# Linear attention with a two-layer MLP: two heads side by side as 64-wide tiles of the TensorE array

## The chip, the cores and the metric

One core of one Trainium2 chip. The metric is the device time of the whole program in microseconds, as the median of several runs. Runs are compared in the state called fast; runs that lay more than 1.5% above the fastest of their kernel are called slow, and neither the medians nor the ratios below include them. The sessions of experiments ran on different chips, so a ratio is always against runs of the kernel before in the same session, and a difference between medians of two sessions is rougher than a ratio.

## The reference, cut to what matters

Blockwise linear attention (batch 4, 8 heads, 768 positions, head size 64) carries a 64x64 state per batch and head. Its output goes through two matrix products with a gated activation between them.

```python
for b in range(nb):
    intra = np.einsum('bhic,bhjc->bhij', qb, kb) * Dmask[None]
    intra = np.einsum('bhij,bhjd->bhid', intra, vb)
    inter = np.einsum('bhid,bhde->bhie', qb * lam_pow[None], kv_state)
    out[:, :, sl] = intra + inter
    kv_state = lam_block[...] * kv_state + np.einsum('bhsd,bhse->bhde', kb_dec, vb)
...
x = attn_out.transpose(0, 2, 1, 3).reshape(B * S, H * D)     # 3072 x 512
h = x @ w_in                                                  # 512 -> 2048
return (h * (1.0 / (1.0 + np.exp(-1.702 * h)))) @ w_out       # 2048 -> 512
```

## The kernel before

The sequence is cut into six windows of 128 positions, 0 to 5. In each window the attention of the next window runs on TensorE between the MLP matmuls of the current one. Window 0 and 1 work in units of one batch and four heads (`u_` functions), windows 2 to 5 in pairs of heads over all four batches (`p_` functions). Two heads of 64 fill the 128 partitions.

```python
def hd(h):
    return slice(64 * h, 64 * h + 64)
...
v_sb = [const.tile([P, NP, B, 3, D], bf16, ...) for i in range(2)]   # v of head 0, zeros, v of head 1
kv_sb = [const.tile([P, NP, B, P], bf16, ...) for i in range(2)]     # states: two 64x64 blocks on the diagonal, zeros else
...
def p_score(w, p):                       # 64-row matmuls, one per head
    ...
    nc.tensor.matmul(s[:, h, b, :], t[hd(h), 0, b, :], t[hd(h), 1, b, :], start=True, stop=True)

def p_kv(w, p):                          # full width: computes both heads' blocks and two unused ones
    ...
    for b in range(B):
        nc.tensor.matmul(t[:, b, :], ks[:, 0, b, :], v_sb[w % 2][:, p, b, 0:3:2, :], start=True, stop=True)
    for h in range(2):                   # the two diagonal blocks, 64 partitions each
        nc.vector.scalar_tensor_tensor(new[hd(h), p, :, hd(h)], old[hd(h), p, :, hd(h)], ..., t[hd(h), :, hd(h)], ...)

def p_out(w, p):                         # full width: the zeros of kv_sb keep the heads apart
    ...
    for b in range(B):
        nc.tensor.matmul(o[:, b, :], kq_of[w, p][:, 1, b, :], kv_sb[w % 2][:, p, b, :], start=True, stop=True)   # inter
        for h in range(2):
            nc.tensor.matmul(o[:, b, hd(h)], sm[:, h, b, :], v_sb[w % 2][:, p, b, 2 * h, :], start=False, ...)   # intra

def u_out(w, b, g):                      # window 1: the same with the operands swapped, 128 columns moving
    ...
    if w:
        nc.tensor.matmul(o[:, p, :], kv_sb[w % 2][:, pp, b, :], kq_of[w, b][:, 1, pp, :], start=True, stop=False)
    for h in range(2):                   # v with a block of zeros beside it
        nc.tensor.matmul(o[:, p, :], v_sb[w % 2][:, pp, b, h : h + 2, :]..., sm[:, h, p, :], ...)
```

## Time and profile before

| | before |
|---|---|
| median of 3 runs | 223.77 us (223.6 to 223.9) |
| profiled span | 222.9 us |
| TensorE (PE) busy | 93% of the span |
| VectorE (DVE), ScalarE (ACT) busy | 41%, 43% |

From the page of the kernel before come the busy times (us, share of the span, number of instructions) and, from its part 4, the chain of work that ended last, by engine:

```profile
PE 208.3 (93%) x1476; PEld 109.0 (49%) x1476; DVE 92.0 (41%) x218; ACT 95.1 (43%) x202; POOL 35.9 (16%) x57
...
PE 74%; DMA 13%; SPq 4%; POOL 3%; DVE 3%; issue 1%; ACT 0%; DVEq 0%; ACTq 0%
```

TensorE bounds the kernel. Of the DMA part of the chain (13%), 11% belong to the first 42 us, in which inputs and weights arrive. The other 2% are the transposing DMA of one output, at 83.5 to 88.1 us. What TensorE waits for after that, from the view of waits between 42 us and the end:

```profile
PE ps_o L337 <- ACT xs L342: 1.6, 1, 1.6
PE ps_t L227 <- DVE kqs L206: 0.6, 1, 0.6
PE ps_s L311 <- DVE sm L318: 0.6, 1, 0.6
PE ps_kv L326 <- DVE kv L329: 0.5, 1, 0.5
PE ps_t L227 <- POOL kqs L206: 0.3, 1, 0.3
```

The columns are the total, the number of waits and the longest. These waits come to 3.6 us in 181 us, and they all lie before 89 us.

The timeline shows what one piece of attention costs. The columns are start, length, engine, line, operation, operands, shape and number. This is one output call (`p_out`) of window 3:

```profile
109.55 1.03 PE L358 MATMUL ps_h<-xT,w_in 128*128 128x512 bf16 x4
110.41 0.22 PE L337 MATMUL ps_o<-kv,kq 128*128 128x128 bf16 x1
110.47 0.22 PE L339 MATMUL ps_o<-v_sb,sm 128*128 128x64 bf16 x2
110.52 0.22 PE L337 MATMUL ps_o<-kv,kq 128*128 128x128 bf16 x1
...
110.86 0.81 PE L358 MATMUL ps_h<-xT,w_in 128*128 128x512 bf16 x3
```

Read the starts, not the lengths: the matmuls overlap in this view, and their ends are modelled by the profiler. From start to start, 128 moving columns take about 56 ns, 64 columns 28 ns and 512 columns 216 ns. The call of 12 matmuls takes 0.45 us. "128\*128" is the part of the array in use, rows by columns. Figures in ns here and below are differences of starts in the packed trace, which has them to 1 ns; the view rounds to 10.

The same view of scores and state matmuls of one pair of heads:

```profile
104.34 0.59 PE L358 MATMUL ps_h<-xT,w_in 128*128 128x512 bf16 x2
104.87 0.40 PE L311 MATMUL ps_s<-kq 64*128 64x128 bf16 x8
105.20 0.40 PE L326 MATMUL ps_kv<-v_sb,kqs 128*128 128x128 bf16 x4
105.43 0.59 PE L358 MATMUL ps_h<-xT,w_in 128*128 128x512 bf16 x2
```

The two MLP matmuls from 104.34 us fill the array until 104.34 + 2 x 0.216 = 104.77 us, but the scores (64 rows) start at 104.87 us. About 0.1 us is empty although nothing is waited for, and the same happens from the scores to the state matmuls. From the state matmuls (128\*128) to the MLP there is no such hole. In what follows such a change of the array's shape is called a passage.

One output call of window 1 (`u_out`) and its two state matmuls, all of one shape:

```profile
55.77 0.22 PE L284 MATMUL ps_o<-kq,kv 128*128 128x128 bf16 x1
55.83 0.27 PE L287 MATMUL ps_o<-sm,v_sb 128*128 128x128 bf16 x2
...
56.11 0.28 PE L262 MATMUL ps_kv<-v_sb,kqs 128*128 128x128 bf16 x2
56.22 0.60 PE L358 MATMUL ps_h<-xT,w_in 128*128 128x256 bf16 x4
```

### The profile page before, as it was taken

The page shows a single profiled execution, that of the slowest core. Times are in us where ns is not written, and L with a number is a line of the kernel's source. Part 1 is how long each engine was busy: PE and PEld are TensorE (multiplying, and loading weights), DVE is VectorE, ACT ScalarE, POOL GpSimd, SP SyncE. Part 2 cuts the span into 40 slices and gives each one's busy share as a digit, 9 for nine tenths or more (in the row PEclk, how much of TensorE's full clock was granted, in tenths as well). Part 3 has the DMA queues.
Part 4 walks back from the last instruction along what each step waited for, and adds up shares of the span by engine and source line. Part 5 has one row for each costly group of instructions (what it writes and reads, how often), then busy time and mean ns, then how long its engine had stood idle before and what let it go on. Part 6 is the DMA issues. An engine that isn't in the chain of part 4 may idle for free.

```text
span 222.9 us, 3886 instructions
## 1 busy us (share of the span) xinstructions
PE 208.3 (93%) x1476; PEld 109.0 (49%) x1476; DVE 92.0 (41%) x218; ACT 95.1 (43%) x202; POOL 35.9 (16%) x57
## 2 busy tenths in 40 slices
PE   7687999699899987999999999999999999999993
PEld 2354344145784675444555444554444545444452
DVE  0792000246588984163654183572372432100121
ACT  5996662244771344146522056612076421366000
POOL 4879300232211001011020120110120000000000
PEclk9999999889999999999999999999999999999999
DMA  6999999899988797889774999747793122200112
GB/s 136 245 206 148 205 206 219 189 232 234 222 187 268 170 238 159 184 222 195 174 167 131 225 239 196 163 109 192 177 252 75 26 84 80 94 3 0 47 47 94
DMA packets 109638, 35.91 MB, mean 161 GB/s; under 512 B 102324, under 2 KB 106676, under 8 KB 109620
## 3 DMA queue, kind: packets, MB, share of 16 engines
q1 hardware_dynamic: 105236, 31.47, 60.7%
q0 software_dynamic: 4240, 4.19, 11.8%
q8 instruction: 11, 0.18, 0.4%
q14 instruction: 7, 0.06, 0.1%
q10 hardware_dynamic: 144, 0.00, 0.0%
HBM read 27.27 MB, written 6.29 MB: 151 GB/s over the span
## 4 chain that ended last, share of the span: by engine, by line
PE 74%; DMA 13%; SPq 4%; POOL 3%; DVE 3%; issue 1%; ACT 0%; DVEq 0%; ACTq 0%
PE ps_out L379 34%; PE ps_h L358 29%; DMA w_out<-in_moe_w_out_dram 7%; DMA qf<-in_q_dram 4%; SPq L82 4%; DMA xT<-xs 2%; PE ps_s L311 2%; POOL w_in L161 2%; PE ps_o L337 2%; PE ps_out L397 2%; PE ps_o L339 2%; PE ps_kv L326 2%; POOL kqs L206 1%; PE ps_t L227 1%; PE ps_s L246 1%
## 5 line engine op out<-in xcount | busy, mean ns | idle before, releaser
L358 PE MATMUL ps_h<-xT,w_in 128*128 128x512 bf16 (+1 forms) x448 | 88.5, 349 | 1.5 <-DMA w_in<-in_moe_w_in_dram 1.5
L379 PE MATMUL ps_out<-w_out,g_sb 128*128 128x512 bf16 x368 | 86.0, 384 | 0.0
L364 ACT ACTIVATE g_sb<-ps_h 128x512 bf16<-128x512 f32 (+1 forms) x112 | 59.5, 537 | 60.2 <-PE ps_h L358 59.2
L358 PEld LDWEIGHTS <-w_in 128*128 128x128 bf16 x448 | 42.1, 98 | 38.9 <-DMA w_in<-in_moe_w_in_dram 2.2
L379 PEld LDWEIGHTS <-g_sb 128*128 128x128 bf16 x368 | 34.5, 98 | 37.9 <-issue 1.0
L386 DVE COPY o_sb<-ps_out 128x512 f32<-128x512 f32 x19 | 13.1, 691 | 56.8 <-PE ps_out L379 50.2
L318 DVE TENSOR_TENSOR sm<-ps_s,dmask 128x512 bf16<-128x512 f32 x32 | 20.6, 686 | 26.9 <-PE ps_s L311 26.9
L300 POOL CAST v_sb<-vf 128x512 bf16<-128x512 f32 x16 | 12.3, 767 | 100.1 <-DMA vf<-in_v_dram 90.4
L342 ACT CAST xs<-ps_o 128x512 bf16<-128x512 f32 x16 | 9.4, 586 | 25.6 <-PE ps_o L339 23.2
L206 DVE TENSOR_TENSOR kqs<-kf,k_pow 128x256 bf16<-128x256 f32 x16 | 7.5, 469 | 27.6 <-DMA kf<-in_k_dram 23.3
L206 POOL TENSOR_TENSOR kqs<-qf,q_pow 128x256 bf16<-128x256 f32 x16 | 10.2, 641 | 29.4 <-DMA qf<-in_q_dram 26.6
L251 DVE TENSOR_TENSOR sm<-ps_s,dmask 128x512 bf16<-128x512 f32 x16 | 11.1, 691 | 5.3 <-PE ps_s L246 4.8
L329 DVE SCALAR_TENSOR_TENSOR kv<-kv,blk_pow,ps_kv 64x256 bf16<-64x256 bf16 x24 | 11.4, 476 | 0.2
L337 PE MATMUL ps_o<-kv,kq 128*128 128x128 bf16 x64 | 9.0, 220 | 1.6 <-ACT xs L342 1.6
L289 ACT CAST xT<-ps_o 128x256 bf16<-128x256 f32 x16 | 6.0, 375 | 9.7 <-PE ps_o L287 9.5
L298 DVE TENSOR_SCALAR kqs<-kf,k_pow 128x256 bf16<-128x256 f32 x32 | 9.8, 349 | 0.2
L298 DVE TENSOR_SCALAR kqs<-qf,q_pow 128x256 bf16<-128x256 f32 x32 | 9.8, 348 | 0.0
L274 DVE SCALAR_TENSOR_TENSOR kv<-kv,blk_pow,ps_kv 64x64 bf16<-64x64 bf16 x32 | 7.7, 279 | 4.9 <-PE ps_kv L262 4.5
L227 PE MATMUL ps_t<-ident,kqs 128*128 128x128 bf16 x64 | 6.8, 220 | 3.2 <-DVE kqs L206 2.5
L339 PEld LDWEIGHTS <-sm 128*128 128x128 bf16 x128 | 7.9, 98 | 3.2 <-issue 1.8
L211 ACT CAST v_sb<-vf 128x256 bf16<-128x256 f32 x16 | 6.4, 401 | 7.1 <-DMA vf<-in_v_dram 6.9
L339 PE MATMUL ps_o<-v_sb,sm 128*128 128x64 bf16 x128 | 9.0, 193 | 0.0
(54 smaller groups left out, 111.7 us busy)
## 6 DMA issues: line engine op xcount, KB each, us to landing
kf<-in_k_dram SPq DMA_DIRECT2D x48, 128.0 KB, 2.9
qf<-in_q_dram SPq DMA_DIRECT2D x48, 128.0 KB, 3.0
vf<-in_v_dram SPq DMA_DIRECT2D x48, 128.0 KB, 3.0
out_dram<-o_sb SPq DMA_DIRECT2D x23, 256.0 KB, 2.7
w_out<-in_moe_w_out_dram POOLq DMA_DIRECT2D x4, 512.0 KB, 15.8
w_in<-in_moe_w_in_dram POOLq DMA_DIRECT2D x3, 512.0 KB, 9.4
w_in<-in_moe_w_in_dram POOLq DMA_DIRECT2D x2, 256.0 KB, 5.6
kq<-kqs SPq DMA_TRANSPOSE x16, 3.5
```

Of the source, the lines that this page charges most:

```text
L206: eng.tensor_tensor(out.rearrange("s p h d -> s (p h) d"), xf.rearrange("s p h d -> s (p h) d"), tab, op=MUL)
L251: nc.vector.tensor_tensor(sm, s_ps.pop((w, b, g)).rearrange("s h (p t) -> s h p t", t=P)[:, :, 0:2, :], dmask[:, :, gs(g), :], op=MUL)
L298: nc.vector.tensor_scalar(kqs[:, i, :, h, :], loaded[w, "kq"[i], p][:, :, h, :], scalar1=(k_pow, q_pow)[i][:, 2 * p + h : 2 * p + h + 1], ...
L300: nc.gpsimd.tensor_copy(v_sb[w % 2][:, p, :, 0:3:2, :], loaded[w, "v", p])
L318: nc.vector.tensor_tensor(sm[:, h], s[:, h], dmask[:, h, p : p + 1, :].to_broadcast([P, B, P]), op=MUL)
L329: nc.vector.scalar_tensor_tensor(new[hd(h), p, :, hd(h)], old[hd(h), p, :, hd(h)], blk_pow[hd(h), 2 * p + h : 2 * p + h + 1], t[hd(h), :, ...
L337: nc.tensor.matmul(o[:, b, :], kq_of[w, p][:, 1, b, :], kv_sb[w % 2][:, p, b, :], start=True, stop=True)
L339: nc.tensor.matmul(o[:, b, hd(h)], sm[:, h, b, :], v_sb[w % 2][:, p, b, 2 * h, :], start=False, stop=True, skip_group_check=True)
L358: nc.tensor.matmul(t[:, bs[0] * P : bs[1] * P], w_in_sb[j][:, kc, i * P : (i + 1) * P], xT(w)[:, kc, bs[0] : bs[1], :].rearrange("p b t -> ...
L364: nc.scalar.activation(g_tile(w)[:, fc, c], h_ps.pop((w, fc))[:, c], GELU)
L379: nc.tensor.matmul(t, g_of[w][:, fc, g * P : (g + 1) * P], w_out_sb[j][:, fc % CW, :], start=(fc == 0), stop=(fc == FFC - 1))
L386: nc.vector.tensor_copy(o, t)
```

## The change

The intent is to stop multiplying by zeros. States are kept as compact 64x64 blocks, one head in each half of the partitions. The inter product runs as two 64-row matmuls, one per head. State matmuls become two 64-column tiles. The zeros in `v_sb` and `kv_sb` and the four memsets that write them vanish, and VectorE updates both heads' states in one instruction. The Trainium skill, TensorEngine Tiling (Array Packing), Gotcha 1: PSUM Pressure, says that row tiles cannot access one PSUM bank at the same time. So the output of windows 2 to 5 takes two banks, one per head, and the state result shares a bank with the transposes.

```diff
-    v_sb = [const.tile([P, NP, B, 3, D], bf16, name=f"v_sb{i}") for i in range(2)]
-    kv_sb = [const.tile([P, NP, B, P], bf16, name=f"kv{i}") for i in range(2)]
+    v_sb = [const.tile([P, NP, B, 2, D], bf16, name=f"v_sb{i}") for i in range(2)]
+    kv_sb = [const.tile([P, NP, B, D], bf16, name=f"kv{i}") for i in range(2)]
 ... (u_kv and u_kv_up: like p_kv below)
 def u_out(w, b, g):
             if w:
-                nc.tensor.matmul(o[:, p, :], kv_sb[w % 2][:, pp, b, :], kq_of[w, b][:, 1, pp, :],
-                                 start=True, stop=False)
-            for h in range(2):
-                nc.tensor.matmul(o[:, p, :], v_sb[w % 2][:, pp, b, h : h + 2, :].rearrange("p c d -> p (c d)"),
-                                 sm[:, h, p, :], start=(not w and h == 0), stop=(h == 1))
+                for h in range(2):
+                    nc.tensor.matmul(o[hd(h), p, :], kv_sb[w % 2][hd(h), pp, b, :], kq_of[w, b][hd(h), 1, pp, :],
+                                     start=True, stop=False)
+            for h in range(2):
+                nc.tensor.matmul(o[hd(h), p, :], v_sb[w % 2][:, pp, b, h, :], sm[:, h, p, :], start=not w, stop=True)
 def p_kv(w, p):
-        for b in range(B):
-            nc.tensor.matmul(t[:, b, :], ks[:, 0, b, :], v_sb[w % 2][:, p, b, 0:3:2, :], start=True, stop=True)
-        ... (two scalar_tensor_tensor of 64 partitions)
+        for b in range(B):
+            for h in range(2):
+                nc.tensor.matmul(t[hd(h), b, :], kqs_of[w, p][:, 0, b, h, :], v_sb[w % 2][:, p, b, h, :],
+                                 start=True, stop=True)
+        nc.vector.scalar_tensor_tensor(kv_sb[(w + 1) % 2][:, p], kv_sb[w % 2][:, p], blk2[:, p : p + 1], t, ...)
 def p_out(w, p):
-            nc.tensor.matmul(o[:, b, :], kq_of[w, p][:, 1, b, :], kv_sb[w % 2][:, p, b, :], start=True, stop=True)
-            for h in range(2):
-                nc.tensor.matmul(o[:, b, hd(h)], sm[:, h, b, :], v_sb[w % 2][:, p, b, 2 * h, :], ...)
+            for h in range(2):
+                nc.tensor.matmul(o[:, h, b, :], kq_of[w, p][hd(h), 1, b, :], kv_sb[w % 2][hd(h), p, b, :],
+                                 start=True, stop=True)
+            for h in range(2):
+                nc.tensor.matmul(o[:, h, b, :], sm[:, h, b, :], v_sb[w % 2][:, p, b, h, :],
+                                 start=False, stop=True, skip_group_check=True)
 ... (window 1: state matmuls a quarter step later than the output; memsets removed; bank layout)
```

More of the change, by code (lines that the diff above doesn't have):

```diff
@@ L208, in u_cast_v @@
     def u_cast_v(w, b, g, eng):
-        out, xf = v_sb[w % 2][:, gs(g), b, 0:3:2, :], loaded[w, "v", b][:, gs(g)]
+        out, xf = v_sb[w % 2][:, gs(g), b, :, :], loaded[w, "v", b][:, gs(g)]
         if eng is nc.scalar:
@@ L223, in u_turn @@
         if (w, b, g) not in t_ps:
-            t_ps[w, b, g] = ps.tile([P, 2, 2, P], bf16, tag="t", name="ps_t")
+            t = ps.tile([P, 8, P], bf16, tag="t" if w else "mm", bufs=1 if w else 3, name="ps_t")
+            t_ps[w, b, g] = t[:, 0:4, :].rearrange("s (i p) t -> s i p t", i=2)
         src = kqs_of[w, b].rearrange("s i p h d -> s i p (h d)")
@@ L257, in u_kv @@
     def u_kv(w, b, g):
-        t = ps.tile([P, 2, P], f32, tag="kv", name="ps_kv")
+        t = ps.tile([P, W], f32, tag="t", bufs=1, name="ps_kv")[:, 0 : 2 * D].rearrange("s (p d) -> s p d", p=2)
         kv_ps[w, b, g] = t
-        ks = kqs_of[w, b].rearrange("s i p h d -> s i p (h d)")
         for p in range(2):
-            nc.tensor.matmul(t[:, p, :], ks[:, 0, 2 * g + p, :], v_sb[w % 2][:, 2 * g + p, b, 0:3:2, :],
-                             start=True, stop=True)
+            for h in range(2):
+                nc.tensor.matmul(t[hd(h), p, :], kqs_of[w, b][:, 0, 2 * g + p, h, :], v_sb[w % 2][:, 2 * g + p, b, h, :],
+                                 start=True, stop=True)
     def u_kv_up(w, b, g):
@@ L267, in u_kv_up @@
         new, old = kv_sb[(w + 1) % 2], kv_sb[w % 2]
-        for h in range(2):
-            if w == 0:
-                nc.scalar.copy(new[hd(h), gs(g), b, hd(h)], t[hd(h), :, hd(h)])
-            else:
-                for p in range(2):
-                    c = 4 * g + 2 * p + h
-                    nc.vector.scalar_tensor_tensor(
-                        new[hd(h), 2 * g + p, b, hd(h)], old[hd(h), 2 * g + p, b, hd(h)], blk_pow[hd(h), c : c + 1],
-                        t[hd(h), p, hd(h)], op0=MUL, op1=ADD)
+        if w == 0:
+            nc.scalar.copy(new[:, gs(g), b, :], t)
+        else:
+            for p in range(2):
+                pp = 2 * g + p
+                nc.vector.scalar_tensor_tensor(new[:, pp, b, :], old[:, pp, b, :], blk2[:, pp : pp + 1], t[:, p, :],
+                                               op0=MUL, op1=ADD)
     def u_out(w, b, g):
-        o = ps.tile([P, 2, P], f32, tag="o", name="ps_o")
+        o = ps.tile([P, 2, W], f32, tag="o", name="ps_o")[:, 0, 0 : 2 * P].rearrange("s (p t) -> s p t", p=2)
         sm = sm_of.pop((w, b, g))
@@ L299, in p_cast @@
                                         scalar1=(k_pow, q_pow)[i][:, 2 * p + h : 2 * p + h + 1], scalar2=None, op0=MUL)
-        nc.gpsimd.tensor_copy(v_sb[w % 2][:, p, :, 0:3:2, :], loaded[w, "v", p])
+        nc.gpsimd.tensor_copy(v_sb[w % 2][:, p], loaded[w, "v", p])
         kq_of[w, p] = work.tile([P, 2, B, P], bf16, tag=f"kq{p}", name="kq")
@@ L322, in p_kv @@
             return
-        t = ps.tile([P, B, P], f32, tag="kv", name="ps_kv")
-        ks = kqs_of[w, p].rearrange("s i b h d -> s i b (h d)")
+        t = ps.tile([P, W], f32, tag="t", bufs=1, name="ps_kv")[:, 0 : B * D].rearrange("s (b d) -> s b d", b=B)
         for b in range(B):
-            nc.tensor.matmul(t[:, b, :], ks[:, 0, b, :], v_sb[w % 2][:, p, b, 0:3:2, :], start=True, stop=True)
-        new, old = kv_sb[(w + 1) % 2], kv_sb[w % 2]
-        for h in range(2):
-            nc.vector.scalar_tensor_tensor(new[hd(h), p, :, hd(h)], old[hd(h), p, :, hd(h)],
-                                           blk_pow[hd(h), 2 * p + h : 2 * p + h + 1], t[hd(h), :, hd(h)],
-                                           op0=MUL, op1=ADD)
+            for h in range(2):
+                nc.tensor.matmul(t[hd(h), b, :], kqs_of[w, p][:, 0, b, h, :], v_sb[w % 2][:, p, b, h, :],
+                                 start=True, stop=True)
@@ L333, in p_out @@
+        nc.vector.scalar_tensor_tensor(kv_sb[(w + 1) % 2][:, p], kv_sb[w % 2][:, p], blk2[:, p : p + 1], t,
+                                       op0=MUL, op1=ADD)
     def p_out(w, p):
-        o = ps.tile([P, B, P], f32, tag="o", name="ps_o")
+        o = ps.tile([P, 2, W], f32, tag="o", name="ps_o")[:, :, 0 : B * D].rearrange("s h (b d) -> s h b d", b=B)
         sm = sm_of.pop((w, p))
         for b in range(B):
-            nc.tensor.matmul(o[:, b, :], kq_of[w, p][:, 1, b, :], kv_sb[w % 2][:, p, b, :], start=True, stop=True)
@@ L338, in p_out @@
             for h in range(2):
-                nc.tensor.matmul(o[:, b, hd(h)], sm[:, h, b, :], v_sb[w % 2][:, p, b, 2 * h, :],
+                nc.tensor.matmul(o[:, h, b, :], kq_of[w, p][hd(h), 1, b, :], kv_sb[w % 2][hd(h), p, b, :],
+                                 start=True, stop=True)
+            for h in range(2):
+                nc.tensor.matmul(o[:, h, b, :], sm[:, h, b, :], v_sb[w % 2][:, p, b, h, :],
                                  start=False, stop=True, skip_group_check=True)
-        xs = work.tile([P, B, P], bf16, tag="xs", bufs=2, name="xs")
@@ L342, in p_out @@
-        nc.scalar.copy(xs, o)
-        nc.sync.dma_start_transpose(out=xT(w)[:, p], in_=xs.rearrange("p b c -> p (b c)"))
+        xs = work.tile([P, B, 2, D], bf16, tag="xs", bufs=2, name="xs")
+        nc.scalar.copy(xs.rearrange("s b h d -> s h b d"), o)
+        nc.sync.dma_start_transpose(out=xT(w)[:, p], in_=xs.rearrange("p b h d -> p (b h d)"))
     def g_tile(w):
@@ L417 @@
         blk_pow = mk_pow(P, 0, "blk_pow")
-        nc.gpsimd.memset(v_sb[0][:, :, :, 1, :], 0.0)
+        blk2 = const.tile([P, NP], f32)
+        for h in range(2):
+            nc.scalar.copy(blk2[hd(h), :], blk_pow[hd(h), h : 2 * NP : 2])
         N = len(UNITS)
@@ L444 @@
                 u_turn_copy(0, *u, nc.vector)
-            if i == 1:
-                nc.gpsimd.memset(kv_sb[1], 0.0)
             if i == N + 1:
@@ L468 @@
                 load_unit(1, nm, *u)
-        nc.gpsimd.memset(v_sb[1][:, :, :, 1, :], 0.0)
-        nc.gpsimd.memset(kv_sb[0], 0.0)
         for fc in range(3):
@@ L498, in units1 @@
                     side.append((t + 0.5 * step, (u_out, 1, *units[i - 2])))
-                    side.append((t + 0.5 * step, (u_kv, 1, *units[i - 2])))
-                    side.append((t + 0.5 * step, (u_kv_up, 1, *units[i - 2])))
+                    side.append((t + 0.75 * step, (u_kv, 1, *units[i - 2])))
+                    side.append((t + 0.75 * step, (u_kv_up, 1, *units[i - 2])))
         e = len(main)
```

## The prediction

> **What bounds it now.** TensorE. The busy table gives PE 93% of the 222.9 us span (DVE 41%, ACT 43%); in the chain of waits PE holds 74%. Up to about 42 us loads decide (PE idles 2.1 us at 39.2 us for the next q). After that the instruction starts show only four PE gaps over 0.4 us: 0.73, 0.72 and 0.66 us behind DVE or DMA (57-79 us) and 1.77 us at 86.9 us (a transposing DMA); 3.9 us in all. From 89 us PE never waits long, so PE time added there is added to the total.
>
> **What a matmul costs there.** From start to start, warm: 56 ns for 128 moving columns, 28 ns for 64, 216 ns for 512, with the weight load hidden (98 ns each, overlapped). The head-pair score matmuls (64 rows) overlap: the second starts 4 ns after the first. But every passage between 128-row and 64-row matmuls leaves 94-98 ns empty: matmul L358 to score L311, score to state update L326. All such passages show this floor; passages within one shape show 2 ns. The Trainium skill, TensorEngine Tiling (Array Packing), Key Properties, says a change of tiling mode drains the engine; the trace agrees, at about 95 ns for row tiles. Whether a change of column width alone drains, before does not show; I assume it does.
>
> **What the change does**, by these numbers:
> - Output, windows 2-5 (16 calls). Before: four times one 56 ns and two 28 ns matmuls, 0.45 us, no passage. After: per batch a 64-row pair (32 ns), then two full-row matmuls (56 ns), so two passages per batch, eight per call: 4x(32+56)+8x95 = 1.11 us. +0.67 us x16 = **+10.7 us**. Halving the inter work saves 24 ns and pays 190.
> - Output, window 1 (8 calls): 0.34 us before; after 4x60+5x95 = 0.71: **+3.0 us**.
> - State matmuls, window 1 (8 calls): 0.11 to about 0.25 us with two passages of their own: **+1.1 us**.
> - State matmuls, windows 2-4 (12 calls): 4x56 becomes four pairs of 64 columns (about 125 ns) plus one more passage: about 0. The same page (Tile-to-Partition Mapping, Restrictions) says column tiling disables Fast Weight Load; if 64-column loads then take about 53 ns each, unhidden, add 0.2-0.3 us per call and 0.1 per window-1 call: **0 to +5 us**.
> - Window 0: about even, and behind loads.
> - DVE: state updates go from 24x476 and 32x279 ns to half as many: -10 us busy, off the critical path except at three of the gaps. GpSimd: four memsets (5.6 us) vanish, before work that waits for loads: 0.
> - The state result now shares one PSUM bank with window 1's transposes: up to +1 us of waits.
> - Longer PE stretches absorb up to 3 us of the 3.9 us of gaps.
>
> Sum: 10.7+3.0+1.1+2+0.5-3 = about +14 us.
>
> **Predicted: 238 us**, 80% range 232 to 244. Faster by over 2%: 0.03; within 2%: 0.04; slower by over 2%: 0.93.
>
> **What would show it.** Right: in windows 2-5 the output stretch is about 1.1 us per call, with about 95 ns between the inter pair and the intra matmuls; PE's busy share does not fall although DVE's busy falls by about 10 us; the loss grows evenly per window (3-4 us per window from 89 us on), and the matmul stages of 32 matmuls keep their 6.9 us. Wrong: output calls near 0.45 us.
>
> **What would make it wrong.** Column-width changes that do not drain (about 232); slow 64-column weight loads (about 242 or more); passages hidden by a weight load going ahead; the shared bank stalling window 1 more than thought; the removed DVE waits opening more than I counted.

## The result, and the profile after

The changed kernel takes 238.06 us (median of 4 runs, 237.31 to 238.36) against 223.84 us of the kernel before in the same rounds. The ratio is 1.061 (95% interval 1.055 to 1.067): it is slower. Ratios here are the mean time of one kernel's fast runs over that of the other's in the same rounds, so they are not quite the ratio of the medians quoted.

The same two lines of the page of the changed kernel, span 236.7 us:

```profile
PE 225.2 (95%) x1636; PEld 112.7 (48%) x1636; DVE 80.6 (34%) x190; ACT 93.6 (40%) x196; POOL 31.3 (13%) x53
...
PE 88%; DMA 5%; SPq 4%; issue 0%; POOL 0%; DVE 0%; ACT 0%
```

VectorE works 11.4 us less and GpSimd 4.6 us less, as intended. TensorE is listed as busy for 16.9 us more, and its share of the chain rises from 74% to 88%. The view of waits of the changed kernel has no TensorE wait at all after 42 us: the five waits of before are gone. TensorE now comes later to each of them, and VectorE has less to do; the section on why the prediction was right says what of this was tested. The output call of window 3, which answers to the one shown before:

```profile
114.42 0.81 PE L358 MATMUL ps_h<-xT,w_in 128*128 128x512 bf16 x3
115.16 0.20 PE L336 MATMUL ps_o<-kv,kq 64*128 64x64 bf16 x2
115.30 0.23 PE L339 MATMUL ps_o<-v_sb,sm 128*128 128x64 bf16 x2
115.46 0.20 PE L336 MATMUL ps_o<-kv,kq 64*128 64x64 bf16 x2
...
116.27 0.81 PE L358 MATMUL ps_h<-xT,w_in 128*128 128x512 bf16 x3
```

One batch now takes 0.30 us (115.16 to 115.46) where it took 0.11. The 64-row pair occupies the array for about 31 ns, since its second matmul starts 3 ns after the first. But 0.14 us pass from its start to that of the full-row matmuls, and 0.16 us more to the next pair, of which the full-row matmuls fill 56 ns. "64\*128" and "128\*128" alternate eight times in the call. Measured from the end of the preceding MLP matmul's slot to the start of the next MLP matmul, the call went from 0.456 to 1.199 us. All 16 calls agree within 2 ns, except one call of before that held the wait for ScalarE.

Scores and state matmuls after:

```profile
109.17 0.38 PE L358 MATMUL ps_h<-xT,w_in 128*128 128x512 bf16 x1
109.49 0.40 PE L311 MATMUL ps_s<-kq 64*128 64x128 bf16 x8
109.81 0.32 PE L326 MATMUL ps_kv<-v_sb,kqs 128*64 128x64 bf16 x8
110.06 0.60 PE L358 MATMUL ps_h<-xT,w_in 128*128 128x512 bf16 x2
```

Eight 64-column matmuls do take less array time than four full ones. But "128\*64" is now a shape of its own, with a passage to the MLP behind it: 0.25 us from the first state matmul to the MLP, against 0.23 before. The output call of window 1 and its state matmuls, which now stand apart:

```profile
57.77 0.24 PE L285 MATMUL ps_o<-kq,kv 64*64 64x128 bf16 x2
57.94 0.25 PE L288 MATMUL ps_o<-sm,v_sb 128*64 128x128 bf16 x2
58.12 0.24 PE L285 MATMUL ps_o<-kq,kv 64*64 64x128 bf16 x2
58.29 0.25 PE L288 MATMUL ps_o<-sm,v_sb 128*64 128x128 bf16 x2
58.47 0.39 PE L358 MATMUL ps_h<-xT,w_in 128*128 128x256 bf16 x2
58.79 0.25 PE L264 MATMUL ps_kv<-v_sb,kqs 128*64 128x64 bf16 x4
```

This output call has five passages and goes from 0.335 to 0.796 us.

The loss grows evenly. From the chain of before, in order of time (start, length, what):

```profile
96.30 8.63 PE ps_h L358 x40
...
121.49 6.91 PE ps_out L379 x32
...
191.69 13.81 PE ps_h L358 x64
```

and from that of the changed kernel:

```profile
100.92 8.63 PE ps_h L358 x40
...
129.16 6.91 PE ps_out L379 x32
...
205.39 13.81 PE ps_h L358 x64
```

In the chain of before, the runs of MLP matmuls that open the stages with the attention of windows 3, 4 and 5 start at 96.30, 128.40 and 160.49 us, and the last stage, which has no attention, starts at 191.69 us. In the changed kernel these are 100.92, 136.07, 171.22 and 205.39 us, later by 4.6, 7.7, 10.7 and 13.7 us: about 3.0 us in each window. Four output calls of +0.743 us make 2.97 us. In the stretches without attention nothing changed: a run of 32 MLP matmuls takes 6.91 us in both.

### The profile page after: what moved, and what is told of

Its sections match the earlier page's. It is cut to its first block, busy times and chain, and to the rows that moved or that the text cites. A ratio compares the mean times of both kernels' runs of the same rounds, so it can differ in the third digit from the quotient of the medians.

```text
span 236.7 us, 4164 instructions
## 1 busy us (share of the span) xinstructions
PE 225.2 (95%) x1636; PEld 112.7 (48%) x1636; DVE 80.6 (34%) x190; ACT 93.6 (40%) x196; POOL 31.3 (13%) x53
## 4 chain that ended last, share of the span: by engine, by line
PE 88%; DMA 5%; SPq 4%; issue 0%; POOL 0%; DVE 0%; ACT 0%
PE ps_h L358 36%; PE ps_out L379 34%; SPq L82 4%; PE ps_o L339 4%; PE ps_o L336 4%; DMA w_in<-in_moe_w_in_dram 3%; PE ps_s L311 2%; DMA qf<-in_q_dram 2%; PE ps_out L397 1%; PE ps_kv L326 1%; PE ps_o L288 1%; PE ps_o L285 1%; PE ps_t L229 1%; PE ps_s L248 1%; PE ps_kv L264 1%
## 5 line engine op out<-in xcount | busy, mean ns | idle before, releaser
L358 PE MATMUL ps_h<-xT,w_in 128*128 128x512 bf16 (+1 forms) x448 | 91.2, 355 | 3.1 <-DMA w_in<-in_moe_w_in_dram 3.1
L379 PEld LDWEIGHTS <-g_sb 128*128 128x128 bf16 x368 | 33.6, 98 | 37.3
L386 DVE COPY o_sb<-ps_out 128x512 f32<-128x512 f32 x19 | 13.1, 690 | 64.2 <-PE ps_out L379 55.9
L300 POOL CAST v_sb<-vf 128x512 bf16<-128x512 f32 x16 | 13.0, 809 | 107.6 <-DMA vf<-in_v_dram 77.0
L339 PE MATMUL ps_o<-v_sb,sm 128*128 128x64 bf16 x128 | 14.8, 198 | 0.0
L336 PE MATMUL ps_o<-kv,kq 64*128 64x64 bf16 x128 | 13.0, 199 | 0.0
L336 PEld LDWEIGHTS <-kq 64*128 64x128 bf16 x128 | 6.1, 92 | 8.4 <-issue 5.9
L339 PEld LDWEIGHTS <-sm 128*128 128x128 bf16 x128 | 7.3, 97 | 2.5
L219 PE MATMUL ps_f<-zeros 128*128 128x512 bf16 x20 | 7.1, 466 | 1.3 <-DVE zeros L112 1.3
L275 DVE SCALAR_TENSOR_TENSOR kv<-kv,blk,ps_kv 128x64 bf16<-128x64 bf16 x16 | 3.8, 277 | 11.8 <-PE ps_kv L264 11.8
```

The lines of the kernel that those rows point to most:

```text
L300: nc.gpsimd.tensor_copy(v_sb[w % 2][:, p], loaded[w, "v", p])
L336: nc.tensor.matmul(o[:, h, b, :], kq_of[w, p][hd(h), 1, b, :], kv_sb[w % 2][hd(h), p, b, :], start=True, stop=True)
L339: nc.tensor.matmul(o[:, h, b, :], sm[:, h, b, :], v_sb[w % 2][:, p, b, h, :], start=False, stop=True, skip_group_check=True)
L358: nc.tensor.matmul(t[:, bs[0] * P : bs[1] * P], w_in_sb[j][:, kc, i * P : (i + 1) * P], xT(w)[:, kc, bs[0] : bs[1], :].rearrange("p b t -> ...
L379: nc.tensor.matmul(t, g_of[w][:, fc, g * P : (g + 1) * P], w_out_sb[j][:, fc % CW, :], start=(fc == 0), stop=(fc == FFC - 1))
L386: nc.vector.tensor_copy(o, t)
```

## The experiments

Theory: each passage costs about 0.1 us of an idle array, and the loss is their number. Rivals: the half-size matmuls and their weight loads are slow in themselves; there are simply more matmuls (1636 against 1476 recorded); the rearranged PSUM banks make TensorE wait. One more rival, that the empty time is a weight load that is not hidden, can be read from the trace of the changed kernel. Within a shape, a weight load starts about one matmul earlier than the matmul that uses it. At all 240 passages after 47 us it starts only 1 to 5 ns before that matmul, when the hole is at least 88 ns old. So the hole is not the duration of a load. What fills it, such as the emptying of the array, the trace does not show. All kernels below gave correct results. Lengths of calls are measured as above.

### banks_only: the PSUM layout alone

The kernel before with the new bank layout and window 1's later state matmuls, all matmuls full width.

```diff
-            t_ps[w, b, g] = ps.tile([P, 2, 2, P], bf16, tag="t", name="ps_t")
+            t = ps.tile([P, 8, P], bf16, tag="t" if w else "mm", bufs=1 if w else 3, name="ps_t")
+            t_ps[w, b, g] = t[:, 0:4, :].rearrange("s (i p) t -> s i p t", i=2)
-        t = ps.tile([P, B, P], f32, tag="kv", name="ps_kv")
+        t = ps.tile([P, W], f32, tag="t", bufs=1, name="ps_kv").rearrange("s (b d) -> s b d", b=B)
-        o = ps.tile([P, B, P], f32, tag="o", name="ps_o")
+        oo = ps.tile([P, 2, W], f32, tag="o", name="ps_o")
+        o = oo[:, 0].rearrange("s (b d) -> s b d", b=B)
```

Expected:

> The kernel before with only the changed bank layout (state result and window-1 transposes share one PSUM bank, the output takes two banks, window 1's state matmuls half a step's quarter later), all matmuls full width as before. Theory (passages between array shapes cost the time): 223 to 225 us, no new passages. Rival (the shared bank makes TensorE wait): up to 3 us more than before, with PE gaps in front of the state matmuls or transposes between 43 and 78 us.

Measured: 223.65 us, ratio 0.999 (0.993 to 1.005). The bank layout costs nothing that these rounds can show, and this rival falls. This kernel is the base of the next ones.

### dummy_passages: passages without the change

In each output call, one useless matmul of 64 rows and 2 columns stands between the inter and the intra matmuls of a batch. The useful matmuls stay as before.

```diff
             nc.tensor.matmul(o[:, b, :], kq_of[w, p][:, 1, b, :], kv_sb[w % 2][:, p, b, :], start=True, stop=True)
+            nc.tensor.matmul(oo[:, 1, 2 * b : 2 * b + 2], kq_of[w, p][hd(0), 1, b, :], kv_sb[w % 2][hd(0), p, b, 0:2],
+                             start=True, stop=True)
```

Expected:

> banks_only plus one useless 64-row matmul of 2 columns between each full-width inter matmul and its two intra matmuls: 8 passages per output call, the useful matmuls keep their full-width shape. Theory (each passage about 97 ns whatever is computed): the output call of windows 2-5 goes from 0.456 to about 1.25 us, +12.7 us in 16 calls, of which about 2 us disappear in the gap at 87 us: about 234 us. Rival (the half-size matmuls and their weight loads are slow in themselves, or the second output bank is): about 0.50 us per call and 224 to 225 us.

Measured: 236.78 us, ratio 1.057 (1.049 to 1.065). The timeline of one call:

```profile
117.31 0.22 PE L339 MATMUL ps_o<-kv,kq 128*128 128x128 bf16 x1
117.46 0.17 PE L340 MATMUL ps_o<-kv,kq 64*128 64x2 bf16 x1
117.56 0.23 PE L343 MATMUL ps_o<-v_sb,sm 128*128 128x64 bf16 x2
117.63 0.22 PE L339 MATMUL ps_o<-kv,kq 128*128 128x128 bf16 x1
```

Four matmuls of two columns lengthen the call from 0.456 to 1.307 us, or 106 ns for each of its eight passages, the time of the useless matmul included. That reproduces nearly the whole loss without a single useful matmul of another size, so the rival that blames the half-size matmuls falls. The total came out 2 to 3 us above the expectation, and the call's own share of that is 16 x (1.307 - 1.25) = 0.9 us. In the profile, against that of banks_only, TensorE was also 1.0 us behind before the first of these calls, where the two kernels are the same, and the gap at 87 us absorbed 1.6 us in place of 2.

### pout_only: the split output alone

banks_only with only the output of windows 2 to 5 split. The states stay padded and the diagonal blocks are read.

```diff
-            nc.tensor.matmul(o[:, b, :], kq_of[w, p][:, 1, b, :], kv_sb[w % 2][:, p, b, :], start=True, stop=True)
+            for h in range(2):
+                nc.tensor.matmul(o[:, h, b, :], kq_of[w, p][hd(h), 1, b, :], kv_sb[w % 2][hd(h), p, b, hd(h)],
+                                 start=True, stop=True)
 ... (intra matmuls and the copy out of PSUM follow the layout of the two banks)
```

Expected:

> banks_only plus only the split output of windows 2-5 (states stay padded, the diagonal blocks are read). Theory: 1.20 us per call as in the changed kernel, 16 x 0.74 = +11.9 us, less up to 2 us that the gap at 87 us absorbs: 233.5 to 235.5 us; the DVE-bound gaps of 57 to 79 us stay as before. Rival (the loss is mainly window 1 or bank sharing): below 230 us.

Measured: 234.74 us, ratio 1.049 (1.043 to 1.054), 1.200 us per call. This one function holds about 11 us of the loss (234.74 - 223.65).

### grouped_by_4 and grouped_by_2: the same matmuls in another order

The changed kernel, all 64-row matmuls of two or four batches first and then their full-row matmuls. Neither the number nor the shape of any matmul changes, only their order, and with it the number of passages: 2 or 4 per call in place of 8. (`start` is set less often, too. That it costs no hole of its own is seen in the scores, which set it on every matmul and follow each other without one.)

```diff
-        for b in range(B):
-            for h in range(2):
-                nc.tensor.matmul(... inter ..., start=True, stop=True)
-            for h in range(2):
-                nc.tensor.matmul(... intra ..., start=False, ...)
+        for b0 in range(0, B, 4):                    # grouped_by_2: step 2
+            for b in range(b0, b0 + 4):
+                for h in range(2):
+                    nc.tensor.matmul(... inter ..., start=b == b0, stop=True, skip_group_check=True)
+            for b in range(b0, b0 + 4):
+                for h in range(2):
+                    nc.tensor.matmul(... intra ..., start=False, ...)
```

`start` is set on the first inter matmul of each bank and group only. The Trainium skill, PSUM — Partial Sum Buffer, The four PSUM rules, says that a second group's first flag in a bank clears the first group's accumulation bits, so that its next matmul would overwrite instead of adding. Both kernels gave correct results with the flag set once; no run here set it more often in this order.

Expected:

> The changed kernel, the same matmuls and the same number of them, but in each output call of windows 2-5 all eight 64-row inter matmuls first and then all eight full-row intra matmuls: 2 passages per call in place of 8. Theory: call of about 0.56 us (4 pairs at 31, 8 x 28, two passages at about 100), 16 x 0.64 = 10.2 us back: 227 to 229 us. Rival (number and size of matmuls, two output banks): stays at 236 to 238 us.

> As grouped_by_4 but in groups of two batches: 4 passages per output call. Theory (time goes with passages): output call about 0.77 us, halfway in passages between 2 and 6: 16 x 0.43 = 6.9 us less than the changed kernel: about 231 us. Rival (only the first passage of a call costs, or cost goes with the matmuls): 228 or 238 us.

Measured: grouped_by_4 227.65 us, ratio 1.018 (1.012 to 1.023, unclear at the mark of 2%), 0.562 us per call. grouped_by_2 230.96 us, ratio 1.030 (1.024 to 1.036), 0.773 us per call. The call of grouped_by_4 in its timeline:

```profile
116.14 0.29 PE L337 MATMUL ps_o<-kv,kq 64*128 64x64 bf16 x8
116.37 0.41 PE L341 MATMUL ps_o<-v_sb,sm 128*128 128x64 bf16 x8
116.61 0.60 PE L381 MATMUL ps_out<-w_out,g_sb 128*128 128x512 bf16 x2
```

| output call | passages | length, us | whole kernel, us |
|---|---|---|---|
| grouped_by_4 | 2 | 0.562 | 227.65 |
| grouped_by_2 | 4 | 0.773 | 230.96 |
| changed kernel | 8 | 1.199 | 238.06 |

Each passage costs (1.199 - 0.562) / 6 = 106 ns in the call, and (238.06 - 227.65) / (6 x 16) = 108 ns in the total, across sessions. The line through these points gives 0.35 us for the call's matmuls without passages, against 0.456 in the kernel before: the change does save 0.1 us per call, and one passage spends it. The rival that blames the number of matmuls falls too.

### grouped_all: window 1 regrouped as well

The same regrouping in `u_out` on top of grouped_by_4 (3 passages per call in place of 5; `start=p == 0` for the inter matmuls).

```diff
-        for p in range(2):
-            ... inter of p, then intra of p
+        for p in range(2):
+            ... inter of p, start=p == 0
+        for p in range(2):
+            ... intra of p
```

Expected:

> grouped_by_4 plus the same regrouping in window 1's output (3 passages per call in place of 5). Theory: 8 x about 0.2 = 1.6 us less than grouped_by_4: 226 to 227 us, still above the kernel before because 2 + 3 + 3 passages per unit remain that the kernel before has not. Rival: no difference from grouped_by_4.

Measured: 226.35 us, ratio 1.009 (1.003 to 1.015). The window-1 call falls from 0.796 to 0.557 us, which for 8 calls is 1.9 us; the medians differ by 1.3 us.

### kv_beside_out: window 1's state matmuls back behind the output

Output and state matmuls end and begin in the same shape there (128\*64), so putting them together saves two passages per call. The state result, however, shares its bank with the transposes that were issued just before.

```diff
-                    side.append((t + 0.75 * step, (u_kv, 1, *units[i - 2])))
-                    side.append((t + 0.75 * step, (u_kv_up, 1, *units[i - 2])))
+                    side.append((t + 0.5 * step, (u_kv, 1, *units[i - 2])))
+                    side.append((t + 0.5 * step, (u_kv_up, 1, *units[i - 2])))
```

Expected:

> The changed kernel with window 1's state matmuls moved straight behind the output (as in the kernel before): both are 128 rows by 64 columns, so two passages per call fall away, 8 x about 0.2 = 1.6 us. Theory A (passages alone): about 236.5 us. Theory B (the shared bank makes the state matmuls wait for the copy of the transposes): waits of 0.3 us or more in front of each of the 8 calls, no gain or up to 2 us worse, 237.5 to 240 us.

Measured: 237.19 us, ratio 1.060 (1.052 to 1.068): not told apart from the changed kernel. The trace shows both effects, the second in fewer calls than Theory B said. Output and state matmuls together take 0.857 us where they took 0.796 + 0.277 us apart. Two of the eight calls waited for the bank, in the view of waits from 42 us on (other lines left out):

```profile
PE ps_kv L264 <- ACT kq L236: 0.5, 2, 0.2
```

By the starts of the matmuls the hole between output and state matmuls is 0.43 us longer in those two calls than in an undisturbed one. So the shared bank does have a price, but only in two calls; the total cannot separate it from the saved passages.

### pkv_only: only the state matmuls of windows 2 to 4 as 64-column pairs

```diff
-            nc.tensor.matmul(t[:, b, :], ks[:, 0, b, :], v_sb[w % 2][:, p, b, 0:3:2, :], start=True, stop=True)
+            for h in range(2):
+                nc.tensor.matmul(t[hd(h), b, hd(h)], kqs_of[w, p][:, 0, b, h, :], v_sb[w % 2][:, p, b, 2 * h, :],
+                                 start=True, stop=True)
```

Expected:

> banks_only plus only the state matmuls of windows 2-4 as pairs of 64-column tiles (12 calls). Theory from the trace of the changed kernel: the four pairs take 0.145 us in place of 0.224, one more passage costs about 0.1: +10 ns per call, within 0.3 us of banks_only. Rival (64-column weight loads are slow): +0.2 us or more per call, +2.4 us.

Measured: 223.13 us, ratio 0.996 (0.990 to 1.002). Scores and state matmuls of a pair take 0.670 us against 0.660 in banks_only. Neither gain nor loss: what the pairs save, the new passage takes.

### inter_with_scores: split matmuls where the shape is already there

The scores are 64\*128 matmuls anyway, with a passage on either side. This kernel (banks_only otherwise) puts the 64-row inter pairs of one pair of heads straight behind the scores of the next, and their intra matmuls behind the full-row state matmuls. That adds no passage for three pairs of heads of four.

```diff
                     side.append((t, (p_score, w, p)))
+                    if p:
+                        side.append((t, (p_inter, w, p - 1)))
                     side.append((t, (p_mask, w, p)))
                     side.append((t, (p_kv, w, p)))
-                if p:
+                if 0 < p < NP:
+                    side.append((t, (p_out, w, p - 1)))
+                elif p:
+                    side.append((t + 0.5 * step, (p_inter, w, p - 1)))
                     side.append((t + 0.5 * step, (p_out, w, p - 1)))
 ... (new p_inter: the 64-row pairs of pout_only, all four batches; p_out keeps the intra matmuls and the copy)
```

Expected:

> A version meant to beat both: banks_only (window 1 full width, padded states), and in windows 2-5 the inter matmuls as 64-row pairs straight behind the 64-row score matmuls of the next pair of heads, then state and intra matmuls full-row. Passages per pair of heads stay at 2 for three of four pairs (4 for the last). Theory: each of 12 such pairs saves 4 x (56-31) = 0.1 us, each of 4 last pairs loses about 0.1: 0.5 to 1 us less than before, 222.7 to 223.5 us. Rival: later evacuation of the output or the wait for the output's banks gives it back: 224 to 226 us.

Measured: 222.77 us, ratio 0.996 (0.991 to 1.002). A repetition was to narrow that.

> The kernel of inter_with_scores once more, unchanged, to narrow its interval against the kernel before. Theory: ratio 0.993 to 0.998. Rival (it was chance): 1.0 or above.

Measured: 222.75 us, ratio 0.995 (0.991 to 0.999). The timeline of one slot:

```profile
110.47 0.40 PE L312 MATMUL ps_s<-kq 64*128 64x128 bf16 x8
110.71 0.28 PE L341 MATMUL ps_o<-kv,kq 64*128 64x64 bf16 x8
110.92 0.40 PE L327 MATMUL ps_kv<-v_sb,kqs 128*128 128x128 bf16 x4
111.15 0.40 PE L349 MATMUL ps_o<-v_sb,sm 128*128 128x64 bf16 x8
```

From scores to inter there is no hole. The whole slot takes 1.009 us where the two separate ones of before took 0.660 + 0.456. Three such slots of a window gain 0.11 us each, and the last pair's call (0.562 in place of 0.456) loses as much once. This is the same split that cost 11 us above, and here it is worth about half a per cent: well below 2%, and only in the repetition does the interval lie below 1.

### inter_later: two matmul groups later

```diff
-                full(m + 1, m + 10, w + 1, 3.0)
+                full(m + 1, m + 12, w + 1, 3.0)
```

Expected:

> inter_with_scores with the score matmuls of windows 2-5 two matmul groups later. In the trace of inter_with_scores the first scores of window 3 waited 0.8 us for the transposed keys and queries at 103 us. Theory: that wait goes and the first scores of window 2 wait less for VectorE too, 0.8 to 1.5 us less: 221.3 to 222.3 us. Rival (the later output makes the next window's first matmuls wait for it): no gain.

Measured: 222.85 us (five fast runs), ratio 0.997 (0.992 to 1.002), no gain over inter_with_scores; the expectation was missed. The profile of this kernel fell in a slow run. In it the wait at 103 us is gone and another one of 2.2 us stands at 90 us, for ScalarE; whether the fast runs have it was not seen, so where the saved wait went stays open.

## Why the prediction was right

It said 238 us and gave this sum; the right-hand column is measured in the traces. "Calls" are TensorE time from slot end to slot start.

| term | predicted, us | measured, us |
|---|---|---|
| output, windows 2-5, 16 calls | +10.7 | 16 x (1.199 - 0.456) = +11.9 |
| output, window 1, 8 calls | +3.0 | 8 x (0.796 - 0.335) = +3.7 |
| state matmuls, window 1 | +1.1 | +1.1 |
| state matmuls, windows 2-4 | 0 to +5, taken as +2 | 12 x 0.010 = +0.1 |
| shared bank | up to +1, taken as +0.5 | no wait after 42 us |
| gaps absorbed | -3 | -3.7 (all four, by the starts of matmuls) |
| sum | +14 | +13.1; the spans differ by 13.7 |

- **The mechanism holds.** Passages were read from the kernel before, where 94 to 98 ns lay between scores and their neighbours. dummy_passages makes them without the change, and the grouped kernels take them away without changing a matmul.
- **"Whether a change of column width alone drains ... I assume it does"** was right as to the time; that it is a drain, the trace does not show. From 128\*128 into 128\*64 the trace shows 95 ns, and back 102 to 103 ns after the state matmuls. (These holes include the 2 ns that also lie between matmuls of one shape.)
- **The passage was sized a little too small.** 95 ns was put in; in alternation a passage costs 106 ns on average. In the output call of windows 2 to 5 the holes are 100 ns into the 64-row pair and 105 to 107 ns out of it, and the second full-row matmul after the hole comes 10 to 11 ns late as well, which the prediction did not count. In window 1, where 64\*64 and 128\*64 alternate, the holes are 116 to 122 ns. This is the missing 1.2 and 0.7 us.
- **The weight-load term was mis-sized.** The prediction allowed 0 to 5 us for 64-column loads that are not hidden, because the Trainium skill, TensorEngine Tiling (Array Packing), Restrictions, says column tiling disables Fast Weight Load. In the trace of the changed kernel, the second pair of 64-column state matmuls starts 53 ns after the first, but the third and fourth follow at 31 ns, and the 12 calls cost 10 ns each in all.
- **The saving on VectorE did not show in the total.** The prediction put it off the critical path except at the gaps. Those gaps are gone in the changed kernel. For the longest, the wait for ScalarE at 87 us, TensorE's later arrival is enough: it is gone in dummy_passages and pout_only too, which keep VectorE's old work. For the gaps of 57 to 79 us, VectorE's shorter work and TensorE's later arrival were not tested apart: pout_only still has the two waits of window 2 (0.5 us each), but there TensorE comes no later to them. The memsets on GpSimd were not tested by themselves.
- **Luck.** The errors nearly cancel: +1.9 us on the output terms against -1.9 us on the state matmuls of windows 2 to 4, -0.5 us on the shared bank and -0.7 us on the gaps. The start-up is luck too. Both kernels run the same 848 MLP matmuls in the same order. Compared by the same one of them, the changed kernel is 4.8 us behind when the kernel before is at 23 us, and only 0.2 us at 46 us, since the kernel before idles 2.1 us at 39.5 us and then runs at a granted clock of 0.57 from 42 to 46 us. In banks_only the same matmul comes 1.9 us earlier than in the kernel before.
- The other 0.6 us between the sum and the spans are found by the same comparison: these 0.2 us at 46 us, 0.3 us because the second MLP matmul behind a column tile comes 10 ns late as well (25 times net), and a hole of 0.1 us between MLP matmuls at 60.8 us of the changed kernel.

## What to carry to other kernels

In this kernel, splitting a zero-padded matmul into two array tiles saved tens of nanoseconds, and every change of the array's shape cost about 100 ns, for a useless matmul of two columns as for useful ones. So count passages before counting multiplications: order the work so that matmuls of one shape stand together, and split only where the shape in question is already in use next door. And where TensorE bounds the kernel, work taken off the other engines need not show: 11.4 us less on VectorE did not show in this total.

## What the Trainium skill lacked or had wrong

- TensorEngine Tiling (Array Packing), Key Properties, says that a change of tiling mode drains the engine but gives no size. Here it is 94 to 98 ns between 128\*128 and 64\*128, 92 to 122 ns where the columns change, and 106 ns on average in alternation. Its list When to Use Tiling names small dimensions as the reason to tile without this price; here the tiled output call lost 0.743 us and saved 0.1.
- The same page says that column tiling excludes Fast Weight Load, and TensorE: Matmul & The Clock Gate, LDWEIGHTS, gives columns / 1.2 as the time of a load in ns, 53 ns for 64 columns. Here the records of the 64-column loads last 102 to 113 ns, longer than the 92 to 99 ns of the 128-column ones, but they overlap: only the second pair of a group starts 53 ns after the first; the further pairs of 64-column matmuls, two loads to a pair, follow at 31 to 32 ns.
- TensorEngine Tiling (Array Packing), Gotcha 1: PSUM Pressure (row tiles and one PSUM bank), is too wide as it stands: in window 1 of the changed kernel the two 64\*64 tiles of the heads write one bank in different partitions, their starts 4 ns apart, and the results are correct.
- TensorE: Matmul & The Clock Gate, Back-to-back issue gap, gives about 81 ns per matmul of 128 columns and about 131 ns for 512 as the sustained pace with weight loads. Here it is 56 and 216 ns, which is what the other formula on that page gives.
